# The second stage of a Fourier transform on one NeuronCore: each batch on its own 64 rows of TensorE, behind the products of u and v

## The chip, the cores and the metric

The kernel runs on one core of one Trainium2 chip. The metric is the device time of one execution in microseconds; the time before is the median of three runs. The profile is that of one further execution, with the records of all engines: TensorE (PE, with its weight loads shown apart as PEld), VectorE (DVE), ScalarE (ACT), GpSimd (POOL) and the queues that issue transfers.

## What is computed

A Fourier mixing layer and a feed-forward layer behind it, both in fp32:

```python
# x: (8, 3008, 256); w_in: (256, 2048); w_out: (2048, 256)
X = np.fft.fft(x, axis=1)
X = np.fft.fft(X, axis=2)
x = X.real.reshape(8 * 3008, 256)
h = x @ w_in
g = h * np.clip(h + 3.0, 0.0, 6.0) / 6.0
out = g @ w_out
```

## The kernel before, in words

**The transform.** The sequence of 3008 is split into 47 x 64. The first stage (`stage1`, L223 to L230, and `stage1_first` for the first pair) is a transform of length 47 over rows; its results (`z`) go through device memory (`zd`). `load_g` fetches them back as a tile `g` with 64 positions of one batch in partitions 0 to 63 and of the other batch in partitions 64 to 127. The second stage (`stage2`, L315) is the transform of length 64 over those positions. The batches are handled in pairs: four pairs, each with `NG` = 6 groups of four values of k1. One call of `stage2` handles two of these four, so there are two calls a group, i = 0 and 1. The transform over the 256 columns is folded into the weights W1 at the start.

**How stage2 computes.** The stationary operand of a product is the data, 128 columns of `g`, over all 128 rows. The moving operand is the table `T`, 128 columns: 64 for each batch. So that each batch meets only its own table, `T` is block-diagonal, with zeros (written once, L688) where the rows of one batch meet the columns of the other. A call makes four such products into one PSUM bank, which one copy on ScalarE (L331) brings to the tile `q`. The two batches of a pair lie in the two halves of the partitions in `stage1` as well: there each product takes 47 of 64 rows and 64 columns of the result, so that four products stand on four different quarters of TensorE's array, in two banks.

**The feed-forward layer.** A chunk has 256 columns; a pair has 12 chunks. A step (p, ck, fc) takes one of eight slices fc of the hidden layer. `mlp1` (L369) makes u and v, two products each (L379), into two of three PSUM buffers with the tag "uv". DVE adds and subtracts (L384, L394, L396), ACT applies the relu (L421), and DVE applies the gate (L424), after which the buffers of u and v are free. `combine` (L426, GpSimd) makes sums of the results, and `mlp2` (L456, products on L464) multiplies seven of them with the output weights. `finish`, `store` and `send` put the results together, turn them (L522) and send them off.

**The order.** It is written out by hand, since `manual_schedule` keeps the instructions of every engine in program order. In a step s of the main loop, TensorE gets first what is listed "ahead" for this step, then the products u and v of step s + 2 (`AHEAD` = 2), then what is listed "behind", then the products of `mlp2` of step s. `beside(p)` fills the two lists. Before, the second stage stands in "ahead" (t + 3 and t + 7, t a multiple of 16 steps), and only `stage1` stands in "behind". In the first eight steps of all, where weights are still being prepared, the loop has another form (`mlp2_first`, then the transfers and weight units that are due).

**PSUM.** Eight banks: one for `bank` after the start (tag "d": stage1, stage2 and the weight preparation take turns), three "uv", four "acc" for `mlp2`. The second product of `stage1` takes a "uv" buffer.

Of the kernel before, what the change touches and what calls it, by code (L numbers as in the profile page):

```python
# [7 lines left out]
F32 = mybir.dt.float32  # L8
# [41 lines left out]
N1, N2 = 47, 64  # L50
# [8 lines left out]
def kernel(  # L59
# [10 lines left out]
    nc = tc.nc  # L70
    P = nc.NUM_PARTITIONS
# [16 lines left out]
    TB = KC * N2  # L88
    NH = N2 // 2 + 1
    NG = NCK // 2  # L90
# [14 lines left out]
    ps_h = ctx.enter_context(tc.tile_pool(name="ps_h", bufs=3, space=PSUM))  # L105
# [13 lines left out]
    T = consts.tile([P, 2, NG, 2, 2 * KK, N2], F32, name="T")  # L119
# [87 lines left out]
    starting = [True]  # L207

    def bank(shape, name):
        if starting[0]:  # L210
            return ps_a.tile(shape, F32, tag="acc", name=name)
        return ps_d.tile(shape, F32, tag="d", name=name)
# [102 lines left out]
    def stage2(pr, gr, i):  # L315

        if i == 0:
            pr.q[gr] = qpool.tile([P, 2, 2 * TB], F32, tag="q", name="q")
        g = pr.g[gr]
        ps = bank([P, 2, TB], "ps2")  # L320
        for u in range(2):
            kk = 2 * i + u

            nk = NH if (gr, kk) == (NG - 1, 2 * KK - 1) else N2
            n = u * P + 2 * nk
            for blk in range(2):

                nc.tensor.matmul(ps[:, blk, u * P:n].rearrange("p (b k) -> p b k", b=2),  # L328
                                 g[:, kk, blk * (P + 1):blk * (P + 1) + P],
                                 T[:, :, gr, blk, kk, 0:nk], start=True, stop=True)  # L330
        nc.scalar.copy(pr.q[gr][:, :, i * TB:i * TB + n], ps[:, :, 0:n])  # L331
# [37 lines left out]
    def mlp1(ch, fc):  # L369
        gr, of, nq = ch.ck // 2, ch.ck % 2 * TB, ch.nq  # L370
        q, qn = ch.pr.q[gr], ch.pr.qn[gr]
        u = ps_h.tile([P, 2, TB], F32, tag="uv", name="u")
        v = ps_h.tile([P, 2, TB], F32, tag="uv", name="v")
        for blk, ps in ((0, u), (1, v)):

            r = slice(0, P - blk)
            for i in range(2):
                f = fc + i * NF
                nc.tensor.matmul(ps[:, i, 0:nq], W1[r, blk, f * P:(f + 1) * P], q[r, blk, of:of + nq],  # L379
                                 start=True, stop=True)  # L380
        s = spool.tile([P, 2, TB], F32, tag="s", name="s")
        for i in range(2):
            f = fc + i * NF
            nc.vector.scalar_tensor_tensor(s[:, i, 0:nq], qn[:, of:of + nq], WN[:, f:f + 1], u[:, i, 0:nq],  # L384
                                           op0=AL.mult, op1=AL.add)


        a = apool.tile([P, 2, 2, TB], F32, tag="a", name="a")
        t = spool.tile([P, 2, 2, TB], F32, tag="t", name="t")
        ch.a[fc] = a  # L390
        if ch.last:
            activate_last(a, t, s, u, v, nq)
            return
        nc.vector.tensor_tensor(u[:], s[:], v[:], op=AL.add)  # L394
        relu(t[:, 0], u[:], 1.0 / 6.0)
        nc.vector.tensor_tensor(v[:], v[:], s[:], op=AL.subtract)  # L396
        relu(t[:, 1], v[:], -1.0 / 6.0)
        gate(a[:, 0], t[:, 0], u[:])
        rev, tk, vk = (m.rearrange("p i (k n) -> p (i k) n", n=N2) for m in (a[:, 1], t[:, 1], v[:]))
        gate(rev[:, :, ::-1], tk, vk)  # L400
# [25 lines left out]
    def combine(ch, fc):  # L426
        a = ch.a[fc][:].rearrange("p m f n -> p (m f) n")[:, :, 0:ch.n]
        c = cpool.tile([P, 4, TB], F32, tag="c", name="c")
        cn = c[:, :, 0:ch.n]

        eng = nc.vector if ch.final and fc == NF - 1 else nc.gpsimd
        add(cn[:, 0:2], a[:, 2:3].to_broadcast([P, 2, ch.n]), a[:, 3::-3], eng)
        add(cn[:, 2], cn[:, 0], a[:, 0], eng)
        add(cn[:, 3], a[:, 1], cn[:, 2], eng)
        ch.c[fc] = cn
# [6 lines left out]
    def mlp2_first(ch, fc):  # L442
        a = ch.a.pop(fc)
        for h in range(2):
            if fc == 0:
                ch.acc[h] = ps_a.tile([P, 2, TB], F32, tag="acc", name="acc")
            for f in range(2):
                nc.tensor.matmul(ch.acc[h][:], G[:, (B11, B12, B21, B22)[2 * f + h], fc, :], a[:, :, f],  # L448
                                 start=(fc == 0 and f == 0), stop=(fc == NF - 1 and f == 1))
        if fc == NF - 1:  # L450
            ch.r = epool.tile([P, 2, 2, TB], F32, tag="r", name="r")
            for h in range(2):
                for m in range(2):
                    nc.scalar.mul(ch.r[:, m, h], ch.acc[h][:, m], (1 - 2 * m) / WS)
# [162 lines left out]
    def mix_w_out(j):  # L617

        g = [block(j, i) for i in range(7)]
        tt = nc.gpsimd.tensor_tensor  # L620
        tt(g[4], g[B22], g[B12], op=AL.subtract)
        tt(g[3], g[B11], g[B12], op=AL.subtract)
        tt(g[5], g[B22], g[3], op=AL.add)
        tt(g[2], g[5], g[B21], op=AL.subtract)
# [60 lines left out]
    for b in range(2):  # L685
        r = slice((1 - b) * N2, (2 - b) * N2)
        t = T[r, b].rearrange("p g a k n -> p g (a k n)")
# [19 lines left out]
    def unit(j):  # L707
        exponent_b(j)
        if j + 1 < len(PIECES):
            head(j + 1)  # L710
        tail(j)
# [10 lines left out]
    def see(x):  # L722
        nc.gpsimd.tensor_copy(seen[:], x)
# [56 lines left out]
    def beside(p):  # L780
        ahead, behind = {}, {}

        def put(t, f, *a, at=ahead):
            at.setdefault(t, []).append((f, a))

        cur = pairs[p]

        late = 4 if p == 0 else 0
        if p == 0:
            put(5, load_g, cur, 1)  # L790
            for gr in range(1, NG):
                put(gr + 1, load_t, gr)
            put(NF - 1, close_w)
            put(NF - 1, nc.sync.dma_start, F[:], c_stage1[:, 0:5 * PB])

        def s2(t, pr, gr):
            for i in range(2):
                put(t + 3 + 4 * i, stage2, pr, gr, i)
            put(t + 8, spread, pr, gr)

        for gr in range(1, NG):
            if gr > 1:
                put(NST * (gr - 2) + 12, load_g, cur, gr)
            s2(NST * (gr - 1) + (late if gr == 1 else 0), cur, gr)
        if p + 1 < NP:
            nx = pairs[p + 1]
            for c in range(NXC):
                t = 2 * late + (9 - late // 4) * c
                put(t, load_x, nx, c)
                put(t + 3, fold, nx, c, 0, nc.gpsimd)  # L810
                put(t + 5, fold, nx, c, 1, nc.gpsimd)
                put(t + 8, stage1, nx, c, at=behind)
            put(NST * (NG - 1) - 2, load_g, nx, 0)
            put(NST * (NG - 1) + 8, load_g, nx, 1)
            s2(NST * (NG - 1), nx, 0)
        return ahead, behind
# [10 lines left out]
    def chunk(s):  # L827
        p, ck, fc = steps[s]
        return chunks[p][ck], fc
# [49 lines left out]
    for s, (p, ck, fc) in enumerate(steps):  # L879
        if ck == 0 and fc == 0:  # L880
            ahead, behind = beside(p)
        for f, a in ahead.get(ck * NF + fc, ()):
            f(*a)
        if s < NF:

            if s in (2, 3):
                (third_step if s == 2 else fourth_step)()
            else:
                mlp1(*chunk(s + 1))
                if s == NF - 1:  # L890
                    combine(*chunk(NF))
                mlp2_first(*chunk(s))
            for dst, src in later[2 * s:2 * s + 2]:
                nc.sync.dma_start(out=dst, in_=src)
            for j in DUE[s]:
                unit(j)

            if s == 5:
                see(chunk(s + 1)[0].a[s + 1][:, 0, 0, 0:1])
                mix_w_out(0)  # L900
                mix_w_out(1)
            if s == NF - 1:
                mlp1(*chunk(NF + 1))
        else:
            if s + AHEAD < len(steps):
                mlp1(*chunk(s + AHEAD))
            for f, a in behind.get(ck * NF + fc, ()):
                f(*a)
            if s + 1 < len(steps):
                combine(*chunk(s + 1))  # L910
            if s < NF + 2:
                mix_w_out(s - NF + 2)
            if prev and fc < 3:
                if fc > 0:
                    store(prev, fc - 1)
                elif not prev.first:
                    finish(prev)
            mlp2(*chunk(s))
        if fc == NF - 1:
            prev = chunks[p][ck]  # L920
# [85 lines left out]
```

## Time and profile before

| what | value |
|---|---|
| time, median of 3 | 1947.92 us (1947.09 to 1950.45) |
| span of the profiled execution | 1945.0 us |
| products u and v (L379), passes | 1536 + 1536 |
| products of mlp2 (L464), passes | 3008 + 2256 |
| products of stage2 (L328), passes | 384, 275 ns each on the page's scale |
| copy of stage2's result (L331) | 48, median 586 ns |
| products of stage1 (L223), passes | 192 |

An fp32 product runs on TensorE as two passes, each with its own weight load, so the counts are twice those of the products in the program; a few records are missing. The ends of products are modelled, and products overlap: the length of one in a group (275 ns) is more than the distance to the next. What a product costs is read from the chain of waits, where a row gives a start, a length and the number of passes. Loads of weights (PEld) overlap products in the same way.

### The profile page before, as it was taken

Reading aid. Unit: us, or ns where it says so; the run is one execution under the profiler, and the core shown is the slowest. Engines: PE = TensorE matmul, PEld = TensorE weight load, DVE = VectorE, ACT = ScalarE, POOL = GpSimd, SP = SyncE. Lnnn points to the kernel's source line nnn. Section 1 sums busy time; section 2 is a strip of 40 time slices with the busy share of each in tenths; the row PEclk is TensorE's granted clock in tenths of the full one; section 3 lists DMA queues with packets and bytes.
Section 4 is the critical chain, followed back from the end, with each engine's and each line's share of the span. In section 5 each row is a group of like instructions: output and inputs, shape, how many; then the busy total and the mean of one; then the engine's idle time right before and its main releaser. Section 6 shows DMA issues by size and latency. Waiting matters only on the chain.

```text
span 1945.0 us, 27925 instructions
## 1 busy us (share of the span) xinstructions
PE 1927.7 (99%) x9254; PEld 1658.3 (85%) x9254; DVE 1437.7 (74%) x2777; ACT 682.5 (35%) x1167; POOL 1416.1 (73%) x1620
## 2 busy tenths in 40 slices
PE   9999999999999999999999999999999999999997
PEld 4678888888998888888898888888899888888887
DVE  6877777777777777777787777777778777777777
ACT  5633333333333333333333333333333333333332
POOL 4078888877688887787678887878666667666664
PEclk9999999999999999999999999999999999999999
DMA  8531312211112132111111221212110101101000
GB/s 235 170 80 40 81 48 57 55 44 31 39 28 55 49 81 57 44 50 31 38 36 45 57 55 44 49 52 52 35 28 20 28 17 27 35 12 28 20 19 20
DMA packets 148959, 96.71 MB, mean 50 GB/s; under 512 B 117791, under 2 KB 131235, under 8 KB 148814
## 3 DMA queue, kind: packets, MB, share of 16 engines
q1 hardware_dynamic: 137350, 58.06, 12.5%
q0 software_dynamic: 10672, 36.67, 6.7%
q8 instruction: 73, 1.20, 0.3%
q14 instruction: 72, 0.59, 0.1%
q10 hardware_dynamic: 792, 0.20, 0.0%
HBM read 57.57 MB, written 37.32 MB: 49 GB/s over the span
## 4 chain that ended last, share of the span: by engine, by line
PE 94%; DVE 3%; ACT 1%; DMA 1%; issue 0%; SPq 0%; DVEq 0%; POOL 0%; ACTq 0%
PE acc L464 56%; PE v L379 16%; PE u L379 16%; PE ps L328 2%; PE ps L223 1%; DVE a L424 1%; PE acc L448 1%; DMA xt<-in_x_dram,IX 1%; DVE s L384 1%; ACT t L421 1%; PE spare L635 0%; DVE o L522 0%; DVE u L405 0%; ACT PM L574 0%; PE ps L278 0%
## 5 line engine op out<-in xcount | busy, mean ns | idle before, releaser
L438 POOL TENSOR_TENSOR c<-a 128x512 f32<-128x512 f32 (+1 forms) x375 | 469.5, 1252 | 363.5 <-PE acc L464 317.5
L464 PE MATMUL acc<-c,G 128*128 128x256 f32 (+1 forms) x3008 | 696.9, 374 | 0.0
L421 ACT ACTIVATE t<-u,half 128x512 f32<-128x512 f32 (+1 forms) x384 | 260.7, 679 | 1143.7 <-DVE u L394 1064.7
L464 PEld LDWEIGHTS acc<-c,G 128*128 128x128 f32 x3008 | 565.4, 190 | 71.1
L384 DVE SCALAR_TENSOR_TENSOR s<-qn,WN,u 128x256 f32<-128x256 f32 (+1 forms) x768 | 330.1, 471 | 333.4 <-PE u L379 332.6
L464 PE MATMUL acc<-a,G 128*128 128x256 f32 (+1 forms) x2256 | 541.2, 375 | 0.0
L464 PEld LDWEIGHTS acc<-a,G 128*128 128x128 f32 x2256 | 421.3, 189 | 71.2 <-issue 17.5
L379 PE MATMUL v<-q,W 127*128 127x256 f32 (+1 forms) x1536 | 389.0, 375 | 2.3 <-DVE a L424 2.3
L379 PE MATMUL u<-q,W 128*128 128x256 f32 (+1 forms) x1536 | 388.0, 375 | 0.0
L424 DVE SCALAR_TENSOR_TENSOR a<-t,u 128x512 f32<-128x512 f32 (+2 forms) x448 | 263.7, 600 | 103.4 <-ACT t L421 99.6
L379 PEld LDWEIGHTS v<-q,W 127*128 127x128 f32 x1536 | 288.3, 190 | 42.1 <-DVE a L424 1.9
L379 PEld LDWEIGHTS u<-q,W 128*128 128x128 f32 x1536 | 285.7, 190 | 35.2 <-issue 0.5
L438 POOL TENSOR_TENSOR c<-a,c 128x256 f32<-128x256 f32 (+1 forms) x375 | 269.0, 717 | 29.4
L438 POOL TENSOR_TENSOR c<-c,a 128x256 f32<-128x256 f32 (+1 forms) x375 | 268.8, 717 | 29.4
L394 DVE TENSOR_TENSOR u<-s,v 128x512 f32<-128x512 f32 x352 | 245.0, 696 | 38.1 <-DVE s L384 1.8
L424 DVE SCALAR_TENSOR_TENSOR a<-t,v 128x512 f32<-128x512 f32 (+1 forms) x480 | 263.4, 565 | 0.2
L421 ACT ACTIVATE t<-v,half 128x512 f32<-128x512 f32 (+1 forms) x384 | 260.6, 679 | 0.5 <-PE acc L464 0.4
L396 DVE TENSOR_TENSOR v<-v,s 128x512 f32<-128x512 f32 x352 | 243.7, 692 | 0.0
L438 POOL TENSOR_TENSOR r<-w,e 128x256 f32<-128x256 f32 (+1 forms) x92 | 88.8, 987 | 3.6
L472 ACT ACTIVATE e<-acc 128x512 f32<-128x512 f32 (+2 forms) x186 | 84.4, 544 | 3.4 <-PE acc L464 3.3
L522 DVE STREAM_TRANSPOSE o<-r 128x256 f32<-128x256 f32 (+1 forms) x192 | 72.5, 415 | 0.2
L438 POOL TENSOR_TENSOR w<-w,e 128x512 f32<-128x512 f32 (+1 forms) x46 | 57.6, 1252 | 3.6
(104 smaller groups left out, 778.0 us busy)
## 6 DMA issues: line engine op xcount, KB each, us to landing
out_dram<-o SPq DMA_DIRECT2D x746, 32.0 KB
zd<-z SPq DMA_DIRECT2D x48, 192.0 KB
g<-zd SPq DMA_DIRECT2D x36, 256.0 KB
xt<-in_x_dram POOLq DMA_DIRECT2D x21, 256.0 KB, 3.7
qn<-qd SPq DMA_DIRECT2D x19, 256.0 KB
st<-in_moe_w_in_dram POOLq DMA_DIRECT2D x8, 512.0 KB, 7.6
st<-in_moe_w_out_dram POOLq DMA_DIRECT2D x8, 512.0 KB, 5.6
xt<-in_x_dram POOLq DMA_DIRECT2D x17, 192.0 KB, 4.0
```

Source lines behind the costliest of these rows:

```text
L223: nc.tensor.matmul(ps[b][h * PB:(h + 1) * PB, 0:n], F[rows(b), 0:PB], y[rows(b), 2 * h:2 * h + n], start=True, stop=not last, skip_group_c ...
L328: nc.tensor.matmul(ps[:, blk, u * P:n].rearrange("p (b k) -> p b k", b=2), g[:, kk, blk * (P + 1):blk * (P + 1) + P], T[:, :, gr, blk, kk, ...
L379: nc.tensor.matmul(ps[:, i, 0:nq], W1[r, blk, f * P:(f + 1) * P], q[r, blk, of:of + nq], start=True, stop=True)
L384: nc.vector.scalar_tensor_tensor(s[:, i, 0:nq], qn[:, of:of + nq], WN[:, f:f + 1], u[:, i, 0:nq], op0=AL.mult, op1=AL.add)
L394: nc.vector.tensor_tensor(u[:], s[:], v[:], op=AL.add)
L396: nc.vector.tensor_tensor(v[:], v[:], s[:], op=AL.subtract)
L421: nc.scalar.activation(t, h, AF.Relu, bias=half[:], scale=scale)
L424: nc.vector.scalar_tensor_tensor(dst, t, 1.0, h, op0=AL.min, op1=AL.mult)
L438: (eng or nc.gpsimd).tensor_tensor(out, in0, in1, op=AL.add)
L464: nc.tensor.matmul(ch.acc[i // 2][:, i % 2, 0:ch.n], G[:, i, fc, :], mv, start=(fc == 0 and i % 2 == 0), stop=(fc == NF - 1), skip_group_c ...
L472: nc.scalar.mul(ch.e[:, k:i + 1, 0:ch.n], ch.acc[i // 2][:, 0:i + 1 - k, 0:ch.n], 1.0 / WS)
L522: nc.vector.transpose(o[:, 0:n // DH, h], ch.r[:, m, h, 0:n].rearrange("p (j i) -> p j i", i=DH))
```

## The change

Each call of `stage2` outside the start, apart from the very last one of a pair (which has fewer columns and keeps its form), makes eight products in place of four. Each takes one batch: 64 rows of `g` and of `T`, 64 columns of `T`. The two batches write to two banks, one from `bank` and one from the "uv" buffers. The zero half of the table is not streamed any more, and products of the two batches stand on different halves of TensorE's rows, so that they can run at the same time. Two copies, one for each bank, bring the results to the same places of `q`. All calls of stage2 in the main loop move from the list "ahead" (steps t + 3, t + 7) to "behind" (t + 2, t + 6), and the first eight steps now work off "behind" as well.

```diff
@@ stage2
         g = pr.g[gr]
+        if not starting[0] and (gr, i) != (NG - 1, 1):
+
+            ps = [t[:, 0:TB].rearrange("p (c u k) -> p c u k", c=2, u=2)
+                  for t in (bank([P, 2 * TB], "ps2"), ps_h.tile([P, 2 * TB], F32, tag="uv", name="ps2"))]
+            for u in range(2):
+                kk = 2 * i + u
+                for blk in range(2):
+                    for b in range(2):
+                        r = slice(b * N2, (b + 1) * N2)
+                        nc.tensor.matmul(ps[b][:, blk, u], g[r, kk, blk * (P + 1):blk * (P + 1) + P],
+                                         T[r, b, gr, blk, kk], start=True, stop=True)
+            q = pr.q[gr][:, :, i * TB:(i + 1) * TB].rearrange("p c (u b k) -> p c u b k", u=2, b=2)
+            for b in range(2):
+                nc.scalar.copy(q[:, :, :, b], ps[b])
+            return
         ps = bank([P, 2, TB], "ps2")
@@ beside
         def s2(t, pr, gr):
             for i in range(2):
-                put(t + 3 + 4 * i, stage2, pr, gr, i)
+                put(t + 2 + 4 * i, stage2, pr, gr, i, at=behind)
             put(t + 8, spread, pr, gr)
@@ main loop, first eight steps
                 mlp2_first(*chunk(s))
+            for f, a in behind.get(fc, ()):
+                f(*a)
             for dst, src in later[2 * s:2 * s + 2]:
```

## The prediction

> **What bounds the kernel now.** I read the page's first two parts, then the chain of waits, then the costliest groups, and last the chain and the timeline of single windows.
>
> ```profile
> PE 1927.7 (99%) x9254; PEld 1658.3 (85%) x9254; DVE 1437.7 (74%) x2777; ACT 682.5 (35%) x1167; POOL 1416.1 (73%) x1620
> ...
> PEclk9999999999999999999999999999999999999999
> ...
> PE 94%; DVE 3%; ACT 1%; DMA 1%; issue 0%; SPq 0%; DVEq 0%; POOL 0%; ACTq 0%
> ```
>
> TensorE (PE) is busy 99% of the span at full clock, and the chain that ended last runs 94% on it. The next engines, VectorE (DVE) and GpSimd (POOL), are under 75%. So a microsecond added to or taken from TensorE's own sequence moves the end by nearly a microsecond. TensorE hardly waits for the others: over the whole span its longest entry is that of v (L379) for the gate (L424) with 2.3 us, 1.5 of them in the start. The weight loads (PEld) are busy 85%, so loads have little room beside the products. The second stage (L328) is 2.2% of the chain.
>
> What a step and both transform stages cost stands in the chain from 575 to 592 us (start, length, what; "x14" counts the passes of TensorE: each fp32 product runs as two, with a weight load for each):
>
> ```profile
> 576.66 3.02 PE acc L464 x14
> 579.68 0.89 PE ps L328 x8
> 580.58 0.87 PE u L379 x4
> ...
> 586.19 0.87 PE v L379 x4
> 587.06 1.02 PE ps L223 x8
> 588.08 3.22 PE acc L464 x14
> ```
>
> A pass of 256 columns takes 3.02 / 14 = 0.216 us, so streaming costs 0.216 x 64 / 256 = 0.054 us for 64 columns, 0.108 for 128 and 0.43 for 512. The second stage's eight passes of 128 columns take 0.89 us, 0.111 each. Streaming and weight loading could both set that figure; two other pieces of the chain say which. In the start, eight passes of one column (pw):
>
> ```profile
> 42.90 0.79 PE pw L643 x8
> ...
> 45.92 0.89 PE ps L339 x8
> ```
>
> One column against 128 saves 0.1 us in eight passes: the seven intervals between them are still 0.113 us each. And the call at 431 us, half of whose passes have 66 columns, takes 0.84 us, but the u products after it take 0.92 in place of 0.87, since their first weights come late: nothing is saved. So **a 128-column weight load sets 0.112 us per pass**, and the second stage stands exactly on that limit.
>
> **What the skill says.** (1) "TensorE: Matmul & The Clock Gate", section LDWEIGHTS (loading the stationary operand): a load's time is its columns over 1.2 GHz, whatever the number of rows. For 128 columns this is 107 ns; the trace has 112. The trace agrees on the rows too as far as it goes: the 47-row, 64-column loads of the first stage take 130 ns each on the page's scale, 94 rows by 96 columns 163, 128 by 128 190, some 30 ns for each 32 columns. (2) "TensorEngine Tiling (Array Packing)", section Key Properties: tiles load and multiply in parallel, and a change of the tiling drains TensorE. The trace shows both at the first stage (L223), which already splits the rows:
>
> ```profile
> 586.99 0.21 PEld L223 LDWEIGHTS ps<-y,F 47*64 47x64 f32 x8 [0.33 <-issue]
> 588.01 1.16 PEld L464 LDWEIGHTS acc<-a,G 128*128 128x128 f32 x6 [0.81 <-issue]
> ```
>
> Eight loads of 130 ns end within 0.21 us, so they ran side by side; and the loader stands idle on both sides of the group. (3) Same page, Gotcha 1: row tiles must write to different PSUM banks. That is why the change takes a second bank from the u/v buffers; before, one bank held both batches.
>
> **Price of a change of tiling.** The first stage adds 1.02 us and makes the step's products longer by 3.22 - 3.02 = 0.20, 1.22 in all. Four tiles side by side stream two passes of 512 columns: 0.86. The exposed first load (64 columns) is 0.112 / 2 = 0.056, the first 128-column load after it 0.112. What is left, 1.22 - 0.86 - 0.056 - 0.112 = 0.19 us, is the two drains. Two numbers of the trace support it: the loader's idle time is put down to issue (waiting for nothing the profile shows), 8.0 us over 24 times before L223 and 17.5 us over 24 times before L464.
>
> **The change, part by part.**
>
> Count: 48 calls of stage2 (4 pairs x 6 groups x 2). Two lie in the start and four keep the old form (last group, second half): 42 calls get the new form.
>
> Removed per call: 8 passes of 128 columns on 128 rows, 0.89 us. Half of what they streamed was the zero half of the block-diagonal table.
>
> Added per call: 8 products, so 16 passes, of 64 columns, each with a 128-column weight load on 64 rows. The loads are still 128 columns wide, since the stationary operand is the data (128 columns of g); their number doubles. If the two row halves load side by side, 8 load intervals remain: 8 x 0.112 = 0.90 us, the first of them exposed because of the drain. Then the last streaming, 0.054, the drains, 0.19, and the exposed load behind, 0.112: **1.25 us**. Only 8 x 0.054 = 0.43 is streamed, hidden behind loads. So the halved columns buy nothing, and the call grows by 1.25 - 0.89 = 0.36 us; 42 x 0.36 = **15.2 us**.
> Bounds of the unknown, which no row of this trace shows for 128-column loads on half the rows: loads one after the other give 16 x 0.112 in place of 8, 0.90 more per call; loads that halve with the rows give 8 x 0.056 in place of 8 x 0.112, 0.45 less. I take side by side, because the eight loads of L223 did that.
>
> Moved: the call from ahead of the next step's u and v to behind this step's. Behind the second-stage products are now queued the 14 passes of mlp2 (L464), not u and v; all are on the same queue, so the sum is the same. The move itself costs nothing.
>
> Added wait: the second bank is one of the three "uv" buffers, so it waits for the gate of the previous step's v; the next u and v wait for the gates of the u and v just made. Queued behind such a wait are mlp2 and the next u and v, that is everything. In the window above, v is finished at 587.06, and by the timeline its u gate ends at 589.49 and its v gate at 590.08. The next u would start at 587.06 + 1.25 + 3.02 = 591.33. So there is over 1 us in hand. stage1 already takes a uv buffer at the same place, and TensorE waited in all 0.8 us for the gates from 520 us on. Nothing.
>
> Evacuation on ScalarE (ACT): one copy of 128x512 (586 ns) becomes two of 128x256 (381 to 406 ns by the rows of L454 and L472), about 0.2 us more per call, 8 us in all on an engine with 65% idle. The copies queue behind the relus of the step just made, which by the timeline end some 2.2 us after v (588.60 + 0.69), so the bank is free about 3.1 us after v; the u that takes it next comes two steps on, over 7 us later, and the group's q is used eight or more steps on. Hidden.
>
> GpSimd, VectorE and the transfers keep their work. Loads of g are wanted at most one step (4.75 us) sooner, and no second-stage product waits for a transfer now: L328's own idle time is 0.5 us of issue.
>
> Sum: 1947.92 + 15.2 = **1963 us**.
>
> **Rivals.**
> A. The row halves load one after the other: 0.36 + 0.90 = 1.26 us per call, 53 us: 2001. For it: the loads here are twice as wide as in L223, where all four tiles differ in rows or columns. Against it: there two tiles shared the rows and still overlapped.
> B. Loads take half the time on half the rows, so streaming and loading fall together: 0.36 - 0.45 = -0.09 us per call, 4 us faster: 1944; if the drains vanish too, 12 us: 1936. For it: the change halves what is streamed. Against: the 47-row loads lie on the line of the columns.
> C. The tiling changes without drains or exposed loads when only the rows are split: the call then costs about its 0.90 us of loads, 0 to 0.06 more than now, and the time is 1948 to 1950. Against: L223's 0.20 us behind it and the idle loader.
> D. The mechanism of the forecast plus waits for uv buffers, up to 0.4 us per call where transposes (0.42 us each) delay the gates: 17 more, 1980. Against: L223's precedent.
>
> **Chances.** Forecast 0.60 (1957 to 1969 as the drains vary by 0.15 us per call), D 0.10, A 0.11, C 0.09, B 0.10. Range 1947 to 1981: it holds the forecast, C and D and leaves out A and B. Within 0.2% is 1944.0 to 1951.8: C and a part of B, 0.10. Faster: 0.09. Slower: the forecast, D and A, 0.81.
>
> **What would show it.** Chain: a second-stage piece of about 1.0 to 1.1 us and 3.22 in place of 3.02 behind it. Timeline: loader idle before L329 and before the following L464. Loads per call 16, in pairs at the same time, pairs 0.11 us apart; 0.11 between single loads is A, pairs 0.06 apart is B, no idle is C. Waits of TensorE on the gates over 5 us would be D. A time under 1944, or weight loads closer than 0.11 us, would prove the forecast wrong.

## The result, and the profile after

The changed kernel takes 1963.72 us (median of 4 runs, 1962.30 to 1964.61) against 1948.49 us in the runs beside it: 15.2 us more, a ratio of 1.0077 with a 95% interval of 1.0062 to 1.0092. That is slower, by the amount forecast.

The page's first part and the shares of the chain, after:

```profile
PE 1942.7 (99%) x9590; PEld 1658.7 (85%) x9590; DVE 1438.4 (73%) x2777; ACT 680.0 (35%) x1209; POOL 1414.4 (72%) x1620
...
PEclk9999999999999999999999999999999999999999
...
PE 93%; DVE 3%; DMA 1%; ACT 1%; issue 1%; SPq 0%; POOL 0%; DVEq 0%; ACTq 0%
```

TensorE is the bound as before. It has 336 passes more (42 calls x 8), and its busy time is up 15.0 us, from 1927.7. The other engines' busy times have hardly moved. Where the time lies is seen in the chain of the changed kernel, from 575 us on (start, length, what, passes):

```profile
581.55 0.86 PE u L394 x4
582.42 0.86 PE v L394 x4
583.28 1.04 PE ps L329 x16
584.32 3.22 PE acc L479 x14
587.54 0.86 PE u L394 x4
```

The second stage (now L329) is a piece of 1.04 us with 16 passes, where a piece of 0.89 with 8 stood, and the products of mlp2 behind it take 3.22 us where they took 3.02. Together 0.15 + 0.20 = 0.35 us per call, and 42 x 0.35 = 14.7 us. The timeline of the weight loads of that call shows why the halved columns save nothing:

```profile
583.21 0.97 PEld L329 LDWEIGHTS ps<-T,g 64*128 64x128 f32 x16 [0.33 <-issue]
```

Sixteen loads of 188 ns (the median of this form) end in 0.97 us. One after the other, 0.112 us apart as before, they would need 15 x 0.112 + 0.188 = 1.87. So they ran two by two: eight pairs, seven intervals of 0.112 between them, and 0.188 for the last. Their starts in the trace show the pairs: 0.01 us from load to load within a pair, 0.11 from pair to pair. In the 0.33 us ahead of them the loader stands idle, and the profile names nothing that it waits for; it is here that the tiling changes. The trace has this 42 times, 14.1 us in all, on L329. It was 0.5 us in all on L328 before.

### The profile page after: what moved, and what is told of

It reads as the page before. It is cut to its first block, busy times and chain, and to the rows that moved or that the text cites. A ratio compares the mean times of both kernels' runs of the same rounds, so it can differ in the third digit from the quotient of the medians.

```text
span 1961.8 us, 28621 instructions
## 1 busy us (share of the span) xinstructions
PE 1942.7 (99%) x9590; PEld 1658.7 (85%) x9590; DVE 1438.4 (73%) x2777; ACT 680.0 (35%) x1209; POOL 1414.4 (72%) x1620
## 4 chain that ended last, share of the span: by engine, by line
PE 93%; DVE 3%; DMA 1%; ACT 1%; issue 1%; SPq 0%; POOL 0%; DVEq 0%; ACTq 0%
PE acc L479 56%; PE v L394 16%; PE u L394 16%; PE ps L329 2%; PE ps L223 1%; DMA xt<-in_x_dram,IX 1%; DVE a L439 1%; DVE s L399 1%; PE acc L463 1%; ACT t L436 1%; PE spare L650 0%; DVE o L537 0%; DVE u L420 0%; ACT PM L589 0%; DMA T<-in_c_stage_dram 0%
## 5 line engine op out<-in xcount | busy, mean ns | idle before, releaser
L479 PEld LDWEIGHTS acc<-a,G 128*128 128x128 f32 x2256 | 417.9, 189 | 71.6 <-issue 17.6
```

The lines of the kernel that those rows point to most:

```text
L479: nc.tensor.matmul(ch.acc[i // 2][:, i % 2, 0:ch.n], G[:, i, fc, :], mv, start=(fc == 0 and i % 2 == 0), stop=(fc == NF - 1), skip_group_c ...
```

## The experiments

The theory, L below: a weight load of 128 columns sets 0.112 us per pass, loads of different row halves run side by side, and going to another tiling and back costs about 0.36 us that nothing hides. The rivals: W, place, waits and copies; S, streaming; P and F, a price of the products themselves. All diffs but one that says otherwise are against the changed kernel; "..." marks what is left out of them.

**All but the split.** Place behind u and v, second bank in a uv buffer, two copies; the products are those of before.

```diff
...
-                    for b in range(2):
-                        r = slice(b * N2, (b + 1) * N2)
-                        nc.tensor.matmul(ps[b][:, blk, u], g[r, kk, ...], T[r, b, gr, blk, kk], ...)
+                    nc.tensor.matmul(ps[u][:, blk], g[:, kk, ...], T[:, :, gr, blk, kk], ...)
...
```

> All of the change but the split: the calls stand behind u and v, write to two banks (one of them a uv buffer) and are copied out by two copies, but the four products take all 128 rows and 128 columns of the block-diagonal table as before. Theory L (weight loads of 128 columns set the pace at 0.112 us, and each change of tiling costs 0.36 us): place, bank and copies cost nothing, 1948.5 us, within 2. Rival W (the new place, the uv buffer's waits or the second copy cost the 15 us): 1963 us.

Measured: 1948.26 us, ratio to before 1.0001 (0.9993 to 1.0009). The chain has the pieces of before in the new place:

```profile
576.97 0.86 PE v L392 x4
577.84 0.89 PE ps L327 x8
578.73 3.02 PE acc L477 x14
```

So the place, the uv buffer and the second copy cost nothing that shows within 2 us. Rival W is out; the whole cost lies in the split.

**The split alone, ahead of u and v.**

```diff
-                put(t + 2 + 4 * i, stage2, pr, gr, i, at=behind)
+                put(t + 3 + 4 * i, stage2, pr, gr, i)
```

> The split products alone, in the place of before: ahead of the next step's u and v (steps t + 3 and t + 7). Theory L: the cost stays, 1964 us, within 2, with drains before u in place of mlp2. Rival W (the place behind u and v is what costs): 1948 us; if the place behind was needed to keep u and v from waiting for the buffer, over 1970 us.

Measured: 1963.05 us, 1.0073 (1.0059 to 1.0086). The price of leaving the tiling moves with it: now it is u that is 0.20 us longer.

```profile
585.54 1.04 PE ps L329 x16
586.58 1.06 PE u L394 x4
```

**Twice the columns.** Each split product streams all 128 columns of its rows of the table.

```diff
...
-                                         T[r, b, gr, blk, kk], start=True, stop=True)
+                                         T[r, :, gr, blk, kk], start=True, stop=True)
...
```

> The changed kernel, but each product on 64 rows streams all 128 columns of its table rows (the zeros again), twice what it needs; the copies take the needed half. Theory L: streaming 128 columns (0.108 us) still hides behind a load (0.112), only the last pass of a call is longer by 0.054: 42 x 0.054 = 2.3 us, 1966 us. Rival S (streaming sets the pace of the split products): 8 x 0.054 = 0.43 more per call, 18 us, 1982 us.

Measured: 1965.24 us, 1.0091 (1.0075 to 1.0106). The call's piece grows from 1.04 to 1.09 us, the 0.054 of its last pass. Rival S is out: the columns that the change takes away were free.

**Eight products on all rows.** 64 columns each, no split, hence no change of tiling.

```diff
-                        nc.tensor.matmul(ps[b][:, blk, u], g[r, kk, ...], T[r, b, gr, blk, kk], ...)
+                        nc.tensor.matmul(ps[b][:, blk, u], g[:, kk, ...], T[:, b, gr, blk, kk], ...)
```

> Eight products of 64 columns per call in the place and banks of the change, but each on all 128 rows, so there is no change of tiling, and the 16 loads of a call all take the same rows. Theory L: 16 x 0.112 = 1.79 us per call in place of 0.89, 42 x 0.90 = 38 us, 1986 us. Rival S (streaming sets the pace): 16 x 0.054 = 0.86 per call, 1948 us.

Measured: 1986.74 us, 1.0192 (1.0176 to 1.0208).

```profile
590.89 1.73 PE ps L329 x16
592.62 3.08 PE acc L479 x14
```

16 loads on the same rows: 1.73 + 0.06 = 1.79 us per call, as worked out. The loader no longer stands idle ahead of each call (0.5 us in all on L329). The passes stream 0.054 us each and still stand 0.112 apart. Side by side, the split kernel needs half of that, so the overlap of the row halves is real and is worth 0.90 us per call; the change spends it on doubling the number of loads.

**One batch after the other.** The four products of one batch first.

```diff
-            for u in range(2):
-                ...
-                    for b in range(2):
+            for b in range(2):
+                for u in range(2):
+                    ...
```

> The changed kernel with the order of the products turned: the four of one batch, then the four of the other, so that neighbours share their rows. Theory L: what runs side by side are neighbours in the queue on different rows. If TensorE keeps products in order, the 16 loads come one after the other, 0.90 us more per call, 38 us, 2001 us; if its queue lets the second batch pass the first, 1964 us as before. Either way the loads of one row half stay 0.112 us apart.

Measured: 1984.03 us, 1.0180 (1.0164 to 1.0195), between the two cases, so neither came. The chain says 1.53 us for the call's piece, 0.49 more than alternating, and 42 x 0.49 = 20.6 us. Busy time in three stretches of one call, the instructions of L329 alone (first the stretch, then busy us and the number of passes and of loads in it):

```profile
588.90:589.45 0.55, 0.48 (x4) 0.48 (x5) 1.00 0.00 0
589.45:589.90 0.45, 0.45 (x10) 0.45 (x9) 1.00 0.00 0
589.90:590.60 0.70, 0.67 (x9) 0.53 (x6) 1.00 0.00 0
```

In the first half microsecond only one batch loads, five loads some 0.11 us apart; then the rate doubles, and at the end four loads 0.11 us apart remain, those of the other batch. (A load that crosses an edge is counted in both stretches.) The second batch starts neither at once nor after the first has ended: its first load starts while three of the first batch's passes, listed ahead of it, have not started. So some passes of one row half can wait without holding up the other half.

**Two and two.**

```diff
             for u in range(2):
                 kk = 2 * i + u
-                for blk in range(2):
-                    for b in range(2):
-                        r = slice(b * N2, (b + 1) * N2)
+                for b in range(2):
+                    r = slice(b * N2, (b + 1) * N2)
+                    for blk in range(2):
```

> The changed kernel with the order two products of one batch, two of the other. When all four of one batch came first, the second batch's first load began after five of the first batch's eight passes had begun, so about three passes of one row half can stand in the queue without holding up the other. If that is the rule (theory D), runs of four passes cost one interval at the start, 0.11 us per call: 1968 us. If only direct neighbours overlap (theory N): one overlap is lost in each run, over 1980 us.

Measured: 1964.36 us, 1.0078 (1.0063 to 1.0094), the time of the alternating order; the call's piece is 1.09 us. Theory N is out. Theory D of this run has the direction, but its cost, 0.11 us per call, was worked out wrongly. By the starts in the trace the second batch does not wait at the beginning of a call (its first load starts 0.01 us after the first batch's), and its next run of four starts 0.06 us late. Both orders fit three waiting passes; that three is the limit is not settled by two orders.

**Half of each load.**

```diff
-                        nc.tensor.matmul(ps[b][:, blk, u], g[r, kk, blk * (P + 1):blk * (P + 1) + P],
+                        nc.tensor.matmul(ps[b][0:N2, blk, u], g[r, kk, blk * (P + 1):blk * (P + 1) + N2],
...
```

> The changed kernel with half of each load left out: 64 of the 128 columns of g are taken, and the results of these 64 are copied to both halves of q, so the output is not the reference's. Rows, columns streamed, place and banks stay. Theory L: 8 x 0.056 + 0.054 + 0.19 + 0.112 = 0.80 us per call in place of 1.25, 42 x 0.45 = 19 us less, 1945 us. Rival F (the extra time is a fixed price of split products, whatever they load): 1964 us.

Measured: 1945.82 us, 0.9983 of before (0.9977 to 0.9990).

```profile
580.32 0.61 PE ps L329 x16
580.93 3.22 PE acc L480 x14
```

The piece falls from 1.04 to 0.61 us, 8 x 0.054 less, with rows, columns streamed and number of passes unchanged. Rival F is out: the width of the load is what most of the call is made of; the 0.20 us behind it stays.

**Groups together, and calls in two.** The first makes the two calls of a group one (19 changes of tiling there and back fewer), the second cuts each call in two (42 more).

```diff
+        if not starting[0] and gr < NG - 1:
+            if i == 1:
+                return
+            ...
+            for kk in range(4):
+                for blk in range(2):
+                    for b in range(2):
+                        ...
```

> The changed kernel with the two calls of a group made as one (16 products, at step t + 2), except in the last group of a pair: 19 fewer changes of tiling there and back, the same products. Theory L: 19 x 0.36 = 7 us less than the changed kernel, 1957 us. Rival P (the extra time lies in the products themselves, not in the change of tiling): 1964 us.

```diff
-            for u in range(2):
+            for u in (v,):
...
                 put(t + 2 + 4 * i, stage2, pr, gr, i, at=behind)
+                if (gr, i) != (NG - 1, 1):
+                    put(t + 3 + 4 * i, stage2, pr, gr, i, 1, at=behind)
```

> The changed kernel with each call cut into two of four products, one step apart: 42 more changes of tiling there and back, the same products. Theory L: 42 x 0.36 = 15 us more than the changed kernel, 1979 us. Rival P (the extra time lies in the products themselves): 1964 us.

Measured: 1955.47 us, 1.0043 (1.0029 to 1.0057), and 1981.98 us, 1.0173 (1.0158 to 1.0189). In the chain, first a group in one call, then half a call:

```profile
558.76 1.93 PE ps L329 x32
560.70 3.22 PE acc L494 x14
```

```profile
587.49 0.59 PE ps L329 x8
588.09 3.22 PE acc L479 x14
```

With the 0.20 us behind each: 2.13 for 32 passes, 1.24 for 16, 0.79 for 8. Each step of 8 passes costs 4 x 0.112 = 0.45 and leaves a rest of about 0.34 per call, whatever its length: the price of a change of tiling. Rival P is out. The time with calls in two is 18 us over the changed kernel where the chain's pieces give 42 x 0.34 = 14. TensorE's busy time has grown by 14.6 of them (1957.3 against 1942.7). The rest is a wait that the changed kernel does not have: twice a half call stands right ahead of the first stage, which then waits until the copies have freed the bank (times in us: in all, how often, longest).

```profile
PE ps L223 <- ACT q L333: 3.7, 2, 1.8
```

**Four quarters.** The experiments point one way: narrower loads, more of them side by side. Split by columns of g as well, each product uses one quarter of the array, as in the first stage; 64-column loads run four at a time.

```diff
-                    for b in range(2):
-                        r = slice(b * N2, (b + 1) * N2)
+                    for h in range(2):
+                        for b in range(2):
+                            r, hs = slice(b * N2, (b + 1) * N2), slice(h * N2, (h + 1) * N2)
+                            o = blk * (P + 1) + h * N2
+                            nc.tensor.matmul(ps[b][hs, blk, u], g[r, kk, o:o + N2],
+                                             T[r, b, gr, blk, kk], start=True, stop=True)
```

> The changed kernel with the columns of the loads split as well: each product takes 64 rows and 64 of the 128 columns of g, so four products stand on four quarters of the array, as in the first stage, and a call makes 16. Nothing is left out. Theory L (a quarter's load takes 0.056 us and the four quarters load side by side): 8 x 0.056 + 0.054 + 0.34 = 0.80 to 0.85 us per call, 1945 to 1947 us. Rival Q (two quarters on the same rows load one after the other): 1.25 us per call as in the changed kernel, 1964 us.

Measured: 1946.13 us, 0.9988 of before (0.9981 to 0.9994).

```profile
556.81 0.62 PE ps L331 x32
557.43 3.22 PE acc L481 x14
```

32 passes take 0.62 us, where 16 passes on halves took 1.04, and 16 passes on two quarters (half of each load) 0.61: quarters that share rows load side by side, and rival Q is out. The call costs 0.82 in place of 0.89. With the two calls of a group together, the price of the tiling is paid once:

```diff
+        if not starting[0] and gr < NG - 1:
+            if i == 1:
+                return
+            ...
+            for kk in range(4):
+                for blk in range(2):
+                    for h in range(2):
+                        for b in range(2):
+                            ...
```

> Four quarters, and the two calls of a group made as one, except in the last group of a pair. Theory L: 16 x 0.056 + 0.054 + 0.30 = 1.25 us per group in place of 1.78 before, 19 x 0.53 = 10 us less than before, and 4 x 0.09 for the single calls: 1938 us. Rival Q: as with the groups together and halves, 1956 us.

Measured: 1939.18 us, 0.9953 (0.9939 to 0.9967). And with the last group of each pair in the same form (the diff is against the kernel just shown):

```diff
-        if not starting[0] and gr < NG - 1:
+        if not starting[0]:
...
+            m = 4 if gr < NG - 1 else 3
...
             for b in range(2):
-                nc.scalar.copy(q[:, :, :, b], ps[b])
+                nc.scalar.copy(q[:, :, :, b], ps[b][:, :, 0:m])
+                if m < 4:
+                    nc.scalar.copy(pr.q[gr][:, :, m * P + b * NH:m * P + (b + 1) * NH], ps[b][:, :, m, 0:NH])
```

> The same, with the last group of each pair in the new form as well (its last products have 33 columns per batch and are copied out by themselves): 23 groups of 1.25 us in the main loop in place of 1.78 (1.74 in the last groups). Theory L: 4 x 0.4 = 1.6 us less than with the last groups in the old form, 1936 us. Rival Q: 1955 us.

Measured: 1937.47 us, 0.9939 of before (0.9926 to 0.9953). The chain and the timeline of the loads of one group:

```profile
553.72 1.09 PE ps L333 x64
554.81 3.22 PE acc L501 x14
```

```profile
553.64 1.02 PEld L333 LDWEIGHTS ps<-T,g 64*64 64x64 f32 x64 [0.33 <-issue]
```

A group of 64 passes takes 1.09 + 0.20 = 1.29 us where two calls took 1.78 before: 23 x 0.49 = 11.3 us, and the medians differ by 11.4. This version beats both kernels. The step from single last groups to this one (1.7 us) is within the intervals of the two ratios.

## Why the prediction was right

- **The bound.** TensorE's own sequence sets the end: it grew by 15.0 us, the time by 15.2. That the forecast, too, was 15.2 to the tenth is luck: the interval of the ratio is 12.1 to 17.9 us, and the pieces of the chain give 14.7.
- **The load limit.** 0.112 us per 128-column load, not streaming, paced the old call and paces the new one: on all rows the interval is the same with 128 columns streamed and with 64. In the new call, doubling the columns moved the call by 0.05 us, halving the load by 0.43. Here the split saves what was free.
- **Side by side.** This was the open term, taken from the first stage's eight loads of 64 columns and bounded on both sides; that it holds for loads twice as wide was not shown before. The trace of after (16 loads in 0.97 us) and eight products on all rows (1.79 us per call) settle it. Rival A's 2001 us would have needed loads one after the other; rival B's 1944 needed loads that shrink with the rows, and 64 rows load as slowly as 128.
- **The price of the tiling.** Expected 1.25 us per call, measured 1.04 + 0.20 = 1.24. The sum of drains, exposed load behind and last pass was put at 0.36; calls of 8, 16 and 32 passes give 0.34. That 0.19 us of it are two drains is worked out only; no run took a drain away by itself. The front one fits the timeline of after:

```profile
582.90 0.38 PE L394 MATMUL v<-q,W 127*128 127x256 f32 x1
583.21 0.33 PE L329 MATMUL ps<-T,g 64*128 64x64 f32 x2
```

The last pass of v starts at 582.90 and streams for 0.216 us, to 583.12; the first split load starts at 583.21, 0.09 us later. The other sign that the prediction named, an idle loader ahead of mlp2 as well, hardly came: the split loads end at 584.18 and the next load starts at 584.25. The 17.5 us over 24 times that the prediction counted as support are 17.6 over 24 times after the change, so they belong to the first stage alone. Rival C, no drain, is out: the loader idles 0.33 us before every call, and 0.34 us per call stays whatever its length.

- **Waits for the uv buffer.** Expected none, and v waits for the gates 2.5 us in all after, 2.3 before. Rival D is out. That the change needs the second bank at all is not shown: no run put both row halves into one.
- **The copies.** Two copies of 375 ns (median) stand in place of one of 586, and the time with all but the split did not move. The 8 us more of busy time were too many: the copies' groups went from 27.7 to 29.9 us, since the two copies of a call overlap. This term was sized too high, off the path.

## What to carry to other kernels

Before splitting TensorE's rows to save streaming, find out what paces the passes: if passes of one column follow each other as slowly as passes of 128, the loads do. A split by rows alone doubles the loads that it runs side by side and then pays for the tiling; a split by rows and columns together halves the load's width too and can pay. Put all products of another tiling into one stretch, since each stretch costs about 0.34 us here, whether it has 8 passes or 32.

## What the runs showed of the hardware

- Loads of 64 rows by 128 columns pace at 0.112 us, as those of 128 rows do; two row halves load at the same time, and four quarters of 64 x 64 as well (64 loads in 1.02 us).
- Overlap depends on the order of the products, but not on direct neighbours: runs of four passes on one row half cost 0.05 us per call against runs of two (one product each), runs of eight cost 0.49.
